# A second MLP's input projection by seven block products instead of eight, with its weights streamed from DRAM

## The chip, the cores and the metric

The kernel runs on one core of a Trainium2 chip. The metric is the device time of one execution in microseconds. Three runs of the kernel before took 1004.17, 1005.59 and 1006.8 us; the median is 1005.59.

## The reference

Three stages follow each other, all in float32. The third is the one that is rewritten.

```python
# attention: q, k, v (4, 8, 576, 64); a query sees its own and the 63 keys before it
x = attention(q, k, v)                       # then seen as (2304 tokens, 512)
# first MLP: 512 -> 1536 -> 512, gated
xn = x / sqrt(mean(x*x) + 1e-6) * rms_g
g = xn @ w_gate
x = (g * sigmoid(g) * (xn @ w_val)) @ w_out
# second MLP: 512 -> 2048 -> 512
h = x @ w_in
out = (h * sigmoid(1.702 * h)) @ w_out2
```

The weights arrive as 64-bit numbers and are turned into float32 on the chip.

## The kernel before, in words

**Precision.** Every large matmul is made of three: an operand is split into a high part (rounded to the matmul's float32r format) and a low part (the rest), and high x high, low x high and high x low are added up in PSUM. So a 128x128 weight tile is used in three matmuls per slice of tokens.

**Tiling.** 2304 tokens are 6 blocks of 384 (`TB`, `NB`). Activations are kept transposed: 512 features are 4 tiles of 128 partitions, tokens run along the free dimension. The first MLP goes over the 6 blocks twice (`ps_i`, each half with 6 of its 12 hidden tiles), since not all its weights fit beside each other; the second half adds to the result of the first (`part`) and evicts it (`x2s`) to DRAM (`x2d`).

**The second MLP, lines 685 to 738.** For each of the 6 blocks, for each of 16 hidden tiles of 128 features: `proj` (L428) does 12 matmuls of 384 columns into `psh` (4 feature tiles by 3 terms); the gate follows, sigmoid on ACT (L711), product on DVE (L712), high part on ACT (L715), low part on DVE (L716); `emit_P` then does 9 matmuls of 512 columns of the hidden tile before (3 slices of 128 tokens by 3 terms) into three accumulators. `psh` alternates between two PSUM banks. At a block's end the accumulators are copied to `ost` (two buffers) and stored.

**Weights.** `w_step` (L149) takes a pair of weight tiles from the queue `w_order`: a load into `st`, two operations on ACT, three on DVE (the conversion), and one step later `w_half` (L139) splits the pair into high and low parts in one of 16 buffers of 8 KB per partition (pool `wp`). The steps are spread by hand over the hidden tiles of the blocks (`extras`, L601). For the second MLP all 32 tiles (16 pairs) then stay in these 16 buffers until the end.

**What sets the order.** A scheduler places the instructions of each engine and assigns buffers; matmuls that go through `on_pe` while `pinned[0]` is set keep the order of the program. All large transfers go through one queue, SP's, in order. PSUM has 8 banks: 4 accumulators, 2 for projections (tags `g` and `v`), 2 for attention.

Of the kernel before, what the change touches and what calls it, by code (L numbers as in the profile page):

```python
# [22 lines left out]
def window_attention__gated_mlp__mlp_kernel(  # L23
# [86 lines left out]
    w_order += [(("h", 0), ("h", 1))]  # L110
    for f in range(2, NF2, 2):
        w_order += [(("h", f), ("h", f + 1)), (("p", f - 2), ("p", f - 1))]
    w_order += [(("p", NF2 - 2), ("p", NF2 - 1))]
# [24 lines left out]

    def w_half():  # L139
        if not half:  # L140
            return
        pair, w24 = half.pop()
        w = wp.tile([128, 2, 1024], F32R, tag="w", name="w")
        nc.scalar.copy(w[:, 0, :], w24.bitcast(F32))
        nc.vector.tensor_tensor(w[:, 1, :], w24.bitcast(F32), w[:, 0, :].bitcast(F32), ALU.subtract)
        for e, key in enumerate(pair):
            weights[key] = w[:, :, e * 512:(e + 1) * 512]
# [380 lines left out]
    if True:  # L528
# [52 lines left out]
        for ps_i in range(2):  # L581
            f_lo, f_hi = ps_i * FH, (ps_i + 1) * FH
            for j in range(NB):
# [17 lines left out]
                def extras(f, i):  # L601
                    s = 3 * (f - f_lo) + i
                    if ps_i == 0:
                        for fn in slots.pop(j * NS + s, ()):
                            fn()
                        if j == 0:
                            if s % 2 == 0:
                                w_step(n_wh)
                        elif s % 9 == 8:
                            w_step(n_w1)  # L610
                    elif not end:
                        if s % 9 == 2:
                            w_step(n_w)
                    else:
                        w_step(n_w)

                pend = None
                for f in range(f_lo, f_hi):
# [33 lines left out]
                    if f == f_lo:  # L652
                        if ps_i == 0 and end:
                            at_es.close()
                            x2p = ctx.enter_context(tc.tile_pool(name="x2p", bufs=1))
                            xr = raw_load(xd[0])
                        elif ps_i == 1:
                            xr = raw_load(x2d[0] if end else xd[j + 1])
# [3 lines left out]
                    if f == f_lo + 3 and (ps_i or end):  # L662
# [16 lines left out]
                if ps_i == 0 and 0 < j and not end:  # L679
# [5 lines left out]
        for i in range(NB):  # L685
            T = blocks2[i][1]
            NTC = T // 128
            acc = [acc_p.tile([128, 512], F32, tag=f"acc{c}", name=f"acc{c}") for c in range(NTC)]

            def emit_P(f, gh, gl):  # L690
                w = weights["p", f]
                terms = [(pi, c) for pi in range(3) for c in range(NTC)]
                if f == NF2 - 1:
                    terms = [(pi, c) for c in range(NTC) for pi in range(3)]
                for pi, c in terms:
                    nc.tensor.matmul(  # L696
                        acc[c],
                        (gh, gh, gl)[pi][:, c * 128:(c + 1) * 128],
                        w[:, (0, 1, 0)[pi], :],
                        start=(f == 0 and pi == 0),  # L700
                        stop=(f == NF2 - 1 and pi == 2),
                    )

            pend = None
            for f in range(NF2):
                while ("h", f) not in weights:
                    w_step(n_w)
                psh = mm_p.tile([128, 512], F32, tag="gv"[f % 2], name="psh")
                proj(psh, weights["h", f], xh, xl, T)
                a = ap_.tile([128, TB], F32, tag="a", name="a")  # L710
                nc.scalar.activation(a[:, :T], psh[:, :T], AF.Sigmoid, scale=1.702)  # L711
                nc.vector.tensor_tensor(a[:, :T], a[:, :T], psh[:, :T], ALU.mult)  # L712
                gh = ap_.tile([128, TB], F32R, tag="ah", name="gh")
                gl = ap_.tile([128, TB], F32R, tag="al", name="gl")
                nc.scalar.copy(gh[:, :T], a[:, :T])  # L715
                nc.vector.tensor_tensor(gl[:, :T], a[:, :T], gh[:, :T].bitcast(F32), ALU.subtract)  # L716
                if i == 0:
                    w_step(n_w)
                if pend is not None:
                    emit_P(*pend)  # L720
                pend = (f, gh, gl)
                if i == 0:
                    w_step(n_w)
                if i + 1 < NB:
                    if f == 2:
                        xr = raw_load(x2d[i + 1])
                    if f == 6:
                        nxh, nxl = raw_split(i + 1, xr)
            emit_P(*pend)
            xh, xl = nxh, nxl  # L730
            for c in range(NTC):
                st = stp.tile([128, 512], F32, tag="os", name="ost", bufs=2)
                if c % 2:
                    nc.vector.tensor_copy(st, acc[c])
                else:
                    nc.scalar.copy(st, acc[c])
                t0 = blocks2[i][0] + c * 128
                nc.sync.dma_start(out=out[t0:t0 + 128, :], in_=st)
# [30 lines left out]
```

## Time and profile before

| | |
|---|---|
| profiled execution, span | 1005.7 us |
| runs, median of 3 | 1005.59 us |
| PE busy | 978.5 us (97%) |
| DVE / ACT busy | 516.3 / 409.6 us |
| DMA | 88.44 MB, mean 88 GB/s |
| mean granted clock of PE | 0.986 |

The profile shows one execution; its span runs from the first to the last instruction, and it states no other time of its own. Three stretches can be told apart: attention with the first half of the first MLP to some 360 us, the second half of the first MLP to 591, and the second MLP to the end. Bytes moved by DMA fall to almost nothing in the last stretch, where all weights are on the chip.

### The profile page before, as it was taken

What the parts mean: (1) busy time and instruction counts of PE and PEld (TensorE: products, weight loads), DVE (VectorE), ACT (ScalarE), POOL (GpSimd) and SP (SyncE); (2) the same over time, 40 slices, a digit from 0 to 9 for tenths busy, and PEclk for the clock granted to TensorE, in tenths of its full rate; (3) what the DMA queues carried; (4) which work ended last, traced back from release to release, by engine and by line L of the source; (5) the groups of instructions that cost most, each with busy time, mean ns of one, the idle gap of its engine ahead of it and who ended that gap; (6) DMA issues with size and microseconds to landing.
All of it is one profiled execution on the core that took longest, in us unless ns stands there. A gap on an engine that the chain in (4) does not pass through costs nothing.

```text
span 1005.7 us, 15601 instructions
## 1 busy us (share of the span) xinstructions
PE 978.5 (97%) x6218; PEld 915.4 (91%) x6218; DVE 516.3 (51%) x1132; ACT 409.6 (41%) x884; POOL 12.2 (1%) x39
## 2 busy tenths in 40 slices
PE   8889999999998999999999999999999999999997
PEld 7888998889998999999999998998999989989996
DVE  5887667676766455665543787242322422322222
ACT  7786565656552333333322464232222322322222
POOL 2000000000000000000000000000000000000000
PEclk9899899999998999999999999999999999999999
DMA  9867445463525231341330541010010100000000
GB/s 223 244 182 207 116 112 155 103 163 101 146 85 168 74 106 45 134 148 73 136 128 9 171 147 50 1 63 1 8 56 1 53 11 1 32 1 1 32 1 32
DMA packets 113321, 88.44 MB, mean 88 GB/s; under 512 B 77664, under 2 KB 104288, under 8 KB 113248
## 3 DMA queue, kind: packets, MB, share of 16 engines
q1 hardware_dynamic: 112720, 87.44, 29.6%
q8 instruction: 49, 0.80, 0.3%
q14 instruction: 24, 0.20, 0.1%
q10 hardware_dynamic: 528, 0.00, 0.0%
HBM read 68.55 MB, written 18.87 MB: 87 GB/s over the span
## 4 chain that ended last, share of the span: by engine, by line
PE 87%; DVE 4%; DMA 3%; SPq 2%; ACT 2%; issue 1%; POOL 0%; DVEq 0%; ACTq 0%
PE acc L696 20%; PE psh L91 20%; PE psg L91 14%; PE psv L91 14%; PE acc L91 14%; SPq L225 2%; PE ps_s L91 1%; PE ps_v L91 1%; PE ps_t L91 1%; DMA qkv<-in_q_dram 1%; SPq L133 1%; DVE m L166 1%; PE ps_r L91 1%; DMA st<-in_moe_w_val_dram 1%; ACT p L321 1%
## 5 line engine op out<-in xcount | busy, mean ns | idle before, releaser
L712 DVE TENSOR_TENSOR a<-a,psh 128x384 f32<-128x384 f32 x96 | 53.1, 554 | 202.2 <-ACT a L711 202.2
L91 PE MATMUL psh<-x2h,w 128*128 128x384 f32 x768 | 153.2, 339 | 0.1
L696 PE MATMUL acc<-w,gh 128*128 128x512 f32 x576 | 152.9, 397 | 0.0
L91 PEld LDWEIGHTS psh<-x2h,w 128*128 128x128 f32 x768 | 137.2, 188 | 3.2 <-DVE a L712 0.4
L711 ACT ACTIVATE a<-psh 128x384 f32<-128x384 f32 x96 | 47.1, 492 | 220.4 <-PE psh L91 217.3
L696 PEld LDWEIGHTS acc<-w,gh 128*128 128x128 f32 x576 | 107.0, 188 | 18.5
L91 PE MATMUL acc<-ah,w 128*128 128x384 f32 x576 | 117.4, 342 | 1.0 <-DVE x2s L673 1.0
L91 PEld LDWEIGHTS acc<-ah,w 128*128 128x128 f32 x576 | 101.5, 188 | 2.7 <-DVE x2s L673 1.3
L627 DVE SCALAR_TENSOR_TENSOR a<-a,psg 128x384 f32<-128x384 f32 x72 | 39.8, 553 | 92.2 <-ACT a L624 92.1
L91 PE MATMUL psh<-x2l,w 128*128 128x384 f32 x384 | 86.2, 338 | 0.0
L696 PE MATMUL acc<-w,gl 128*128 128x512 f32 x288 | 85.1, 396 | 0.0
L716 DVE TENSOR_TENSOR gl<-a,gh 128x384 fp32r<-128x384 f32 x96 | 53.4, 557 | 50.5 <-ACT gh L715 42.7
L624 ACT ACTIVATE a<-psg 128x384 f32<-128x384 f32 x72 | 35.3, 490 | 102.5 <-PE psg L91 102.5
L91 PE MATMUL psg<-xh,w 128*128 128x384 f32 x288 | 70.2, 369 | 6.6 <-ACT xh L423 4.2
L91 PEld LDWEIGHTS psh<-x2l,w 128*128 128x128 f32 x384 | 69.9, 188 | 5.9
L715 ACT CAST gh<-a 128x384 fp32r<-128x384 f32 x96 | 49.3, 513 | 62.6 <-DVE a L712 49.8
L634 ACT CAST ah<-a 128x384 fp32r<-128x384 f32 x72 | 36.9, 513 | 81.9 <-DVE a L631 81.7
L696 PEld LDWEIGHTS acc<-w,gl 128*128 128x128 f32 x288 | 54.2, 189 | 12.5
L91 PE MATMUL acc<-al,w 128*128 128x384 f32 x288 | 63.9, 341 | 0.0
L91 PE MATMUL psv<-xh,w 128*128 128x384 f32 x288 | 62.0, 348 | 0.0
L91 PEld LDWEIGHTS psg<-xh,w 128*128 128x128 f32 x288 | 52.1, 199 | 10.8 <-ACT xh L423 5.0
L91 PE MATMUL psv<-x2h,w 128*128 128x384 f32 x288 | 58.9, 340 | 0.0
(106 smaller groups left out, 1413.4 us busy)
## 6 DMA issues: line engine op xcount, KB each, us to landing
st<-in_moe_w_out_dram SPq DMA_DIRECT2D x28, 512.0 KB, 4.4
o<-x2s SPq DMA_DIRECT2D x48, 192.0 KB, 2.0
st<-in_moe_w_in_dram SPq DMA_DIRECT2D x16, 512.0 KB, 4.6
st<-in_moe_w_gate_dram SPq DMA_DIRECT2D x12, 512.0 KB, 4.0
st<-in_moe_w_val_dram SPq DMA_DIRECT2D x12, 512.0 KB, 5.4
qkv<-in_v_dram SPq DMA_DIRECT2D x20, 256.0 KB, 3.9
x<-xraw SPq DMA_DIRECT2D x6, 768.0 KB, 3.5
xr<-x SPq DMA_DIRECT2D x6, 768.0 KB, 4.2
```

Source lines behind the costliest of these rows:

```text
L91: ins = op(*args, **kw)
L133: nc.sync.dma_start(out=dst, in_=w_src(kind, f))
L166: nc.vector.scalar_tensor_tensor(m.bitcast(U32), hi.bitcast(U32), 0x80000000, m.bitcast(U32), ALU.bitwise_and, ALU.bitwise_or)
L225: nc.sync.dma_start(out=t[off:off + n], in_=src[b, :, s:s + n, :].rearrange("h s d -> s h d"))
L624: tanh = nc.scalar.activation(a, psg[:, :T], AF.Tanh, scale=0.5).ins
L627: nc.vector.scalar_tensor_tensor(a, a, 1.0, psg[:, :T], ALU.add, ALU.mult)
L634: ah_ins = nc.scalar.copy(ah, a).ins
L696: nc.tensor.matmul(acc[c], (gh, gh, gl)[pi][:, c * 128:(c + 1) * 128], w[:, (0, 1, 0)[pi], :], start=(f == 0 and pi == 0), stop=(f == NF2 ...
L711: nc.scalar.activation(a[:, :T], psh[:, :T], AF.Sigmoid, scale=1.702)
L712: nc.vector.tensor_tensor(a[:, :T], a[:, :T], psh[:, :T], ALU.mult)
L715: nc.scalar.copy(gh[:, :T], a[:, :T])
L716: nc.vector.tensor_tensor(gl[:, :T], a[:, :T], gh[:, :T].bitcast(F32), ALU.subtract)
```

## The change

The input projection of the second MLP is rewritten as a product of 2x2 block matrices: two blocks of tokens (rows) by two halves of the 512 features, times two halves of the features by two hidden tiles (`f` and `f + 8`). Strassen's scheme (in Winograd's form) needs seven products of such blocks where the plain way has eight; each is 2 feature tiles by 3 terms, 6 matmuls of 384 columns. Sums and differences of the blocks are formed ahead of the split into high and low parts: of the weights in the first MLP (`w_products`, seven 256-column products per pair of hidden tiles, stored to DRAM as `wid`; the output weights are stored as `wod`), of the tokens once per pair of blocks (`x_operand`, seven operands in `wp` buffers).

The second MLP is now 3 pairs of blocks by 8 rounds. A round loads its weights from DRAM (`wi_load`, `wo_load`, one round ahead), accumulates products in two banks `a` and `b`, and takes copies of partial sums (`snapshot`) to form four gates. The output matmuls of the round before stand between the products, as four groups of nine (`groups`); the first round of a pair of blocks has two groups empty, or all but one in the very first, which gets the first MLP's last output matmuls (`late`). The accumulators are now six banks. PE's order is that of the program.

Shortened diff of the parts that matter:

```diff
-    w_order += [(("h", 0), ("h", 1))]
-    for f in range(2, NF2, 2):
-        w_order += [(("h", f), ("h", f + 1)), (("p", f - 2), ("p", f - 1))]
+    NP2 = NF2 // 2
+    for f in range(NP2):
+        w_order += [(("h", f), ("h", f + NP2)), (("p", f), ("p", f + NP2))]
...
+    def w_products(f, m):
+        b11, b21, b12, b22 = (m[:, i * 256:(i + 1) * 256] for i in range(4))
+        t = wp.tile([128, 4, 256], F32, tag="w", name="wt")
+        nc.vector.tensor_tensor(t[:, 0, :], b12, b11, ALU.subtract)
+        nc.vector.tensor_tensor(t[:, 1, :], b22, t[:, 0, :], ALU.subtract)
+        nc.vector.tensor_tensor(t[:, 2, :], b22, b12, ALU.subtract)
+        nc.vector.tensor_tensor(t[:, 3, :], b21, t[:, 1, :], ALU.subtract)
+        hi = wp.tile([128, 7, 256], F32R, tag="w", name="whi")
+        lo = wp.tile([128, 7, 256], F32R, tag="w", name="wlo")
+        for dst, src in ((slice(0, 2), m[:, 0:512]), (slice(2, 3), m[:, 768:1024]), (slice(3, 7), t)):
+            src = src if src is t else src.rearrange("p (b c) -> p b c", c=256)
+            nc.scalar.copy(hi[:, dst, :], src)
+            nc.vector.tensor_tensor(lo[:, dst, :], src, hi[:, dst, :].bitcast(F32), ALU.subtract)
+        d = dram.tile([128, 2, 7, 256], F32, name=f"wi_{f}", tag=f"wi_{f}")
+        nc.sync.dma_start(out=d[:, 0], in_=hi.bitcast(F32))
+        nc.sync.dma_start(out=d[:, 1], in_=lo.bitcast(F32))
+        wid[f] = d
...
-                    elif not end:
-                        if s % 9 == 2:
-                            w_step(n_w)
-                    else:
+                    elif s % 6 == 2:
                         w_step(n_w)
...
-                if ps_i == 0 and 0 < j and not end:
+                if (ps_i == 0 and 0 < j and not end) or (ps_i and end):
                     late.append(finish)
...
+        pinned[0] = True
...
+        def x_operand(raws, i):
...
+            t = wp.tile([128, 2, 2, TB], F32R, tag="w", name="xop")
+            nc.scalar.copy(t[:, 0], src)
+            nc.vector.tensor_tensor(t[:, 1], src, t[:, 0].bitcast(F32), ALU.subtract)
+            return t
...
+        def wi_load(f):
+            w = [wp.tile([128, 7, 256], F32R, tag="w", name="wi") for _ in range(2)]
+            for e in range(2):
+                nc.sync.dma_start(out=w[e].bitcast(F32), in_=wid[f][:, e])
+            return w
...
+        def product(ps, w, x, first):
+            i = 0
+            for wi, xx in ((0, 0), (1, 0), (0, 1)):
+                for c in range(2):
+                    on_pe(
+                        nc.tensor.matmul,
+                        ps[:, :TB],
+                        w[wi][:, c * 128:(c + 1) * 128],
+                        x[:, xx, c, :],
+                        start=(first and i == 0),
+                        stop=(i == 5),
...
+        def gate(c, g, i):
+            a = ap_.tile([128, TB], F32, tag="a", name="a")
+            nc.scalar.activation(a, c, AF.Sigmoid, scale=1.702)
+            nc.vector.tensor_tensor(a, a, c, ALU.mult)
+            nc.scalar.copy(g[0][:, i, :], a)
+            nc.vector.tensor_tensor(g[1][:, i, :], a, g[0][:, i, :].bitcast(F32), ALU.subtract)
...
+        def evict(sb, row):
+            if row % 3 == 0:
+                ost[0] = stp.tile([128, 3, 512], F32, tag="st", name="ost")
...
+            if f < NP2 - 1:
+                return [lambda q=q: terms([(q, c) for c in range(3)]) for q in (0, 3, 1, 2)]
+            return [lambda: None, lambda: rows(0), lambda: None, lambda: rows(1)]
...
+        groups = [late.pop()] + [lambda: None] * 3
+        for sb in range(NSB):
+            for f in range(NP2):
...
+                if not last:
+                    nwi, nwo = wi_load(f + 1), wo_load(f + 1)
+                elif sb + 1 < NSB:
+                    nwi, nwo = wi_load(0), wo_load(0)
+                if sb + 1 < NSB:
+                    if f == 2:
+                        raws = x_raws(sb + 1)
+                    if f in (4, 5, 6):
+                        i = MADE[f - 4]
+                        nxops[i] = x_operand(raws, i)
...
+                a = mm_p.tile([128, 512], F32, tag="g", name="psa")
+                prod(a, 0, True)
+                s1 = snapshot(a, "ah")
+                groups[0]()
...
+                prod(b, 1, True)
+                prod(a, 5, False)
+                nc.vector.tensor_tensor(s1, s1, b[:, :TB], ALU.add)
+                s2 = snapshot(a, "ah")
+                gate(s1, g, 0)
+                groups[1]()
...
+                prod(b, 6, True)
+                prod(a, 4, False)
+                s4 = snapshot(a, "al")
+                nc.vector.tensor_tensor(s4, s4, b[:, :TB], ALU.add)
+                gate(s4, g, 3)
+                groups[2]()
+                prod(a, 2, False)
+                prod(b, 3, False)
+                gate(a[:, :TB], g, 1)
+                nc.vector.tensor_tensor(s2, s2, b[:, :TB], ALU.add)
+                gate(s2, g, 2)
+                groups[3]()
+                groups = out_groups(sb, f, g, wo)
...
+            if sb + 1 < NSB:
+                for i in MADE[3:]:
+                    nxops[i] = x_operand(raws, i)
```

Where the instructions stand now, at three places. First PE, as the second MLP begins: before, two hidden tiles of block 0 and then the output matmuls of the first (psh is the projection, acc_6152 and acc_6153 two accumulators).

```order
L91 MATMUL psh<-x2h,w 128x384 x8
L91 MATMUL psh<-x2l,w 128x384 x4
L696 MATMUL acc_6152<-w,gh 128x512 x2
L696 MATMUL acc_6153<-w,gh 128x512 x2
L696 MATMUL acc_6152<-w,gl 128x512
L696 MATMUL acc_6153<-w,gl 128x512
```

The same place after the change, from the first MLP's last matmul on (psa and psb are the two banks of products, xop an operand of tokens, wi one of weights, wo the output weights).

```order
L91 MATMUL acc_5975<-al,w 128x384
L91 MATMUL psb<-xop,wi 128x384 x6
L91 MATMUL psa<-xop,wi 128x384 x6
L91 MATMUL psb<-xop,wi 128x384 x6
L91 MATMUL psa<-xop,wi 128x384 x12
L91 MATMUL psb<-xop,wi 128x384 x6
L91 MATMUL psa<-xop,wi 128x384 x6
L91 MATMUL acc<-wo,g 128x512 x9
```

In this first round no output matmuls stand between the products, and two products into bank a follow each other (x12); from the second round on there is a group of nine after the first, third, fifth and seventh product.

Second ACT, in the last block of the first MLP's second half. Before (psg is the gate's projection, ah the high part of the gated hidden tile, w the split of a weight pair, st its conversion):

```order
L624 ACTIVATE a<-psg 128x384
L144 CAST w<-m 128x1024
L634 CAST ah<-a 128x384
L163 ACTIVATE st<-st 128x1024
L164 ACTIVATE st<-st 128x1024
```

After, in the same block (L648 is the tanh, L658 the cast ah, L744 the high parts of the first pair's operands):

```order
L166 CAST w<-m 128x1024
L744 CAST xop<-xr 128x768 x2
L744 CAST xop<-xs 128x768 x2
L648 ACTIVATE a<-psg 128x384
L658 CAST ah<-a 128x384
L744 CAST xop<-xs 128x768 x2
L648 ACTIVATE a<-psg 128x384
L744 CAST xop<-xr 128x768
L658 CAST ah<-a 128x384 x2
```

Four operand casts and the tanh of the next hidden tile now stand between a weight cast and the cast ah.

Third the queue of SP, around the last stores of the first MLP (o_5 is the last block's result). Before:

```order
L450 DMA xr<-o_2_5101 128x1536
L133 DMA st<-in_moe_w_out_dram 128x1024 x2
L676 DMA o_5_6139<-x2s 128x384 x4
L450 DMA xr<-o_3_5432 128x1536
```

After (wi and wo are the streamed weights of a round):

```order
L753 DMA wi<-wi_4280 128x1792 x2
L758 DMA wo<-wo_4397 128x2048
L719 DMA xr<-o_3_5568 128x1536
L753 DMA wi<-wi_4530 128x1792 x2
L758 DMA wo<-wo_4641 128x2048
L753 DMA wi<-wi_4767 128x1792 x2
L758 DMA wo<-wo_4891 128x2048
L700 DMA o_5_6300<-x2s 128x384 x4
```

The loads of the first three rounds stand ahead of the four stores.

## Rows read from the trace of the kernel before

**Rows 1.** The page's first part: busy us, share of the span, instructions, by engine.

```profile
PE 978.5 (97%) x6218; PEld 915.4 (91%) x6218; DVE 516.3 (51%) x1132; ACT 409.6 (41%) x884; POOL 12.2 (1%) x39
```

**Rows 2.** Busy us of each engine (instructions) by stretch, PE clock, DMA share, GB/s.

```profile
362.00:591.40 229.40, 229.40 (x1299) 228.96 (x1298) 130.76 (x213) 81.85 (x125) 0.00 (x0) 1.00 0.33 112
562.00:574.00 12.00, 12.00 (x70) 12.00 (x69) 10.83 (x16) 3.70 (x6) 0.00 (x0) 1.00 0.56 186
591.40:1000.00 408.60, 408.30 (x2030) 367.84 (x2028) 139.86 (x247) 115.77 (x222) 0.00 (x0) 1.00 0.07 24
```

**Rows 3.** The page's groups: line, engine, operation, tiles, count, busy us, mean ns, idle.

```profile
L91 PE MATMUL psh<-x2h,w 128*128 128x384 f32 x768 | 153.2, 339 | 0.1
L696 PE MATMUL acc<-w,gh 128*128 128x512 f32 x576 | 152.9, 397 | 0.0
...
L91 PE MATMUL psh<-x2l,w 128*128 128x384 f32 x384 | 86.2, 338 | 0.0
L696 PE MATMUL acc<-w,gl 128*128 128x512 f32 x288 | 85.1, 396 | 0.0
...
L715 ACT CAST gh<-a 128x384 fp32r<-128x384 f32 x96 | 49.3, 513 | 62.6 <-DVE a L712 49.8
```

**Rows 4.** Timeline, second MLP: start us, us, engine, line, operation, count, idle before.

```profile
703.15 0.87 PE L91 MATMUL psh<-x2l,w 128*128 128x384 f32 x4
...
703.86 1.57 PE L91 MATMUL psh<-x2h,w 128*128 128x384 f32 x8
704.12 0.49 ACT L711 ACTIVATE a<-psh 128x384 f32<-128x384 f32 x1 [2.60 <-PE psh L91]
...
705.27 1.57 PE L696 MATMUL acc<-w,gh 128*128 128x512 f32 x6
...
706.68 0.86 PE L696 MATMUL acc<-w,gl 128*128 128x512 f32 x3
...
707.38 0.87 PE L91 MATMUL psh<-x2l,w 128*128 128x384 f32 x4
```

**Rows 5.** Groups by shape, 362 to 591.4 us, DVE and ACT.

```profile
L166 DVE SCALAR_TENSOR_TENSOR m<-st,m 128x1024 uint32<-128x1024 uint32 x12 | 14.7, 1222 | 0.2
L169 DVE CUSTOM_DVE_ANT_0 m<-st,m 128x2048 uint16<-128x2048 uint16 x12 | 14.6, 1218 | 0.1
...
L144 ACT CAST w<-m 128x1024 fp32r<-128x1024 f32 x12 | 12.6, 1050 | 19.8 <-DVE m L169 18.1 <-PE psv L91 1.6
...
L671 DVE SCALAR_TENSOR_TENSOR x2s<-acc,part 128x384 f32<-128x384 f32 x20 | 10.5, 553 | 4.0 <-PE acc L91 3.0 <-DMA o<-x2s 0.8
L165 DVE TENSOR_SCALAR m<-st 128x1024 uint32<-128x1024 uint32 x12 | 8.3, 692 | 3.8 <-ACT st L163 3.8
```

**Rows 6.** DMA issues: queue, count, KB each, us from issue to landing.

```profile
xr<-o SPq DMA_DIRECT2D x6, 768.0 KB, 4.1
```

**Rows 7.** Timeline of the end.

```profile
998.93 0.86 PE L696 MATMUL acc<-w,gl 128*128 128x512 f32 x3
...
1002.10 0.59 ACT L736 COPY ost<-acc 128x512 f32<-128x512 f32 x1 [2.15 <-DMA out_dram<-ost]
1002.71 0.33 SPq L738 DMA_DIRECT2D out_dram<-ost  x1
```

**Rows 8.** Busy us by stretch, where PE's clock fell and where not.

```profile
320.00:322.00 2.00, 2.00 (x7) 2.00 (x8) 2.00 (x4) 0.00 (x0) 0.00 (x0) 0.50 0.98 280
333.50:336.00 2.50, 1.50 (x7) 0.99 (x6) 1.48 (x3) 0.95 (x3) 0.00 (x0) 1.00 0.23 81
```

**Rows 9.** Timeline of PE around these two places.

```profile
318.03 0.44 PE L91 MATMUL psg<-xh,w 128*128 128x384 f32 x1 [1.30 <-ACT xh L423]
319.89 2.61 PE L91 MATMUL psg<-xh,w 128*128 128x384 f32 x7 [1.42 <-DVE xh L421]
...
335.20 1.15 PE L91 MATMUL acc<-ah,w 128*128 128x384 f32 x5 [0.99 <-DVE x2s L673]
```

More of the change, by code (lines that the diff above doesn't have):

```diff
@@ L145, in w_half @@
         nc.vector.tensor_tensor(w[:, 1, :], w24.bitcast(F32), w[:, 0, :].bitcast(F32), ALU.subtract)
+        if pair[0][0] == "p":
+            d = dram.tile([128, 2, 1024], F32, name=f"wo_{pair[0][1]}", tag=f"wo_{pair[0][1]}")
+            nc.sync.dma_start(out=d, in_=w.bitcast(F32))
+            wod[pair[0][1]] = d
+            return
         for e, key in enumerate(pair):
@@ L656, in window_attention__gated_mlp__mlp_kernel @@
                             xr = raw_load(xd[0])
-                        elif ps_i == 1:
-                            xr = raw_load(x2d[0] if end else xd[j + 1])
+                        elif ps_i == 1 and not end:
+                            xr = raw_load(xd[j + 1])
                     if f == f_lo + 1 and ps_i == 1:
@@ new lines, in window_attention__gated_mlp__mlp_kernel, with x_raws @@
+        while w_next[1] < n_w or half:
+            w_step(n_w)
+        pinned[0] = True
+        W_OF = (0, 1, 2, 6, 3, 4, 5)
+        NSB = NB // 2
+        def x_raws(sb):
+            r = [x2p.tile([128, KC, TB], F32, tag=t, name="xr") for t in ("xr", "xh")]
+            for e in range(2):
+                nc.sync.dma_start(out=r[e], in_=x2d[2 * sb + e])
+            sums = x2p.tile([128, 2, 2, TB], F32, tag="xl", name="xs")
+            return [r[0][:, 0:2, :], r[0][:, 2:4, :], r[1][:, 0:2, :], r[1][:, 2:4, :], sums[:, 0], sums[:, 1]]
@@ new lines, in window_attention__gated_mlp__mlp_kernel, with out_term @@
+        accs = {}
+        def out_term(sb, f, g, wo, q, c, pi):
+            e, t = q % 2, q // 2
+            row = 3 * t + c
+            on_pe(
+                nc.tensor.matmul,
+                accs[sb][row],
+                g[(0, 0, 1)[pi]][:, q, c * 128:(c + 1) * 128],
+                wo[:, (0, 1, 0)[pi], e * 512:(e + 1) * 512],
+                start=(f == 0 and q == 3 * t and pi == 0),
+                stop=(f == NP2 - 1 and q == 1 + t and pi == 2),
+            )
+        def evict(sb, row):
+            if row % 3 == 0:
+                ost[0] = stp.tile([128, 3, 512], F32, tag="st", name="ost")
+            st = ost[0][:, row % 3, :]
+            if row % 2:
+                nc.vector.tensor_copy(st, accs[sb][row])
+            else:
+                nc.scalar.copy(st, accs[sb][row])
+            t0 = sb * 2 * TB + row * 128
+            nc.sync.dma_start(out=out[t0:t0 + 128, :], in_=st)
@@ new lines, in window_attention__gated_mlp__mlp_kernel, with out_groups, terms, rows @@
+        ost = [None]
+        def out_groups(sb, f, g, wo):
+            def terms(todo):
+                for q, c in todo:
+                    for pi in range(3):
+                        out_term(sb, f, g, wo, q, c, pi)
+            def rows(t):
+                for c in range(3):
+                    terms([(3 * t, c), (1 + t, c)])
+                    evict(sb, 3 * t + c)
+            if f == 0:
+                banks = [(acc_p, f"acc{c}") for c in range(4)] + [(atp, "att")] * 2
+                accs[sb] = [pool.tile([128, 512], F32, tag=tag, name="acc") for pool, tag in banks]
+            if f < NP2 - 1:
+                return [lambda q=q: terms([(q, c) for c in range(3)]) for q in (0, 3, 1, 2)]
+            return [lambda: None, lambda: rows(0), lambda: None, lambda: rows(1)]
@@ L742 @@
+        for fn in groups:
+            fn()
 _INS = ["q", "k", "v", "moe_w_gate", "moe_w_val", "moe_w_out", "moe_rms_g", "moe2_w_in", "moe2_w_out"]
```

103 lines of the change are left out of this document (52 added, 51 removed).

## The prediction

> **What bounds the kernel now.** I read the page's first part, then the busy time by stretch, then the costliest groups, then the timeline of a few microseconds in the stretch that the change rewrites. The first part shows PE busy for 978.5 of 1005.7 us [rows 1]; the next busiest engine has half of that. A busy PE may still be waiting inside its pipeline, so the share alone says little. The stretch of the second MLP, 591.4 to 1000, says more: PE 408.3 of 408.6 us at clock 1.00, DVE 140, ACT 116, DMA 24 GB/s [rows 2]. The groups give the count of its matmuls: 768 + 384 into psh with 384 columns, 576 + 288 into acc with 512 [rows 3]. The duration of one (339 or 397 ns) is a latency and overlaps its neighbours; the price is the distance between starts. In the timeline [rows 4] 12 matmuls of 384 go from 703.15 to 705.27, 0.1767 us each, and 9 of 512 from 705.27 to 707.38, 0.2344 each: one hidden tile of one block takes 4.23. 96 of these are 406.1; the 12 matmuls of 384 columns that the first MLP leaves to this stretch are 2.1; together 408.2 of 408.6. So there is nothing in it but the matmul stream, and a matmul less is its whole distance less, as long as nothing else comes late.
>
> **The change, part by part.** *Products.* A round (two blocks, two hidden tiles) had 48 input matmuls and has seven products of six: 42. There are 24 rounds, so 144 fewer: 144 x 0.1767 = -25.4 us. The output matmuls stay at 864. A new round lasts 42 x 0.1767 + 36 x 0.2344 = 15.86 us. Six-matmul runs cost nothing extra by the same rows: the change from 384 to 512 columns and back is already inside the 4.23.
>
> *Element work in the round.* Three copies on ACT and three additions on DVE come to four gates. No row shows a copy out of a product's bank; the nearest are the gate's cast on ACT, 0.51 [rows 3], and an eviction of 384 columns on DVE, 0.55 [rows 5]. With these DVE has 11 x 0.55 = 6.1 and ACT 11 x 0.5 = 5.5 of 15.86 us, so neither is a bound. What counts is the chain on one bank: PE's last matmul, copy, next product into the same bank. The sigmoid starts 0.26 after PE's next matmul (703.86 to 704.12) [rows 4]; with 0.49 for the copy and an estimated 0.1 until PE goes on it is 0.85. Between a copy and the next product into that bank stand nine output matmuls (2.11) or another product (1.06), so it is hidden, at 0. That cover is missing in the first round of each of the three block pairs, where the group before the third product into bank a is empty, as the order on PE shows (psa x12): 3 x 0.85 = +2.55. In the very first round the second round's first product also waits for the gate that reads bank a, 0.26 + 0.49 + 0.55 + 0.1 = 1.4 behind six matmuls of 1.06, with evictions of the first MLP ahead of it on DVE: +1.0, between 0 and 5 (below, the queue).
>
> *Streamed weights.* A round loads 2 x 0.917 + 1.049 = 2.88 MB, 182 GB/s for 15.86 us. Nothing of before streams so long, but from 562 to 574 the DMA moved 186 GB/s at a share of 0.56, so about 330 at full share, while PE was busy for all 12 us at clock 1.00 and DVE for 10.8 [rows 2]. A load of 768 KB lands 4.1 us after its issue [rows 6]. The 16 weight buffers hold seven operands, the round's three tiles, the output tile of the round before and the next three: 14, so the loads run a round ahead. I put it at 0, between 0 and +10 at the changes of block pair, where the next pair's operands take the spare buffers.
>
> *Preparation in the first MLP.* Each of eight pairs of hidden tiles gets four 256-column subtractions and 768 more columns of low parts on DVE. With 0.55 at 384 columns and 1.22 at 1024 [rows 5] that is 4 x 0.42 + 1.11 = 2.8, 22 in all; of DVE's 140 us in the second MLP 107 are gates (192 x 0.555), and of the other 33 I count half as weight work that moves here; eleven 768-column operations (0.95 each by the same two rows) make the first operands. DVE goes from 131 [rows 2] to about 180 of 229 us. Its 90% beside a PE without a gap from 562 to 574 [rows 2] lets me put this at 0, with one exception, which the order on ACT shows: in the last block a weight cast, four operand casts and the next tanh stand ahead of the cast ah. After the tanh DVE must do 0.55 + 0.69 + 1.22 + 2 x 0.55 + 1.22 = 4.8 before the weight cast can start; then ACT has 1.05 + 4 x 0.83 (estimated between 0.51 and 1.05) + 0.49 + 0.51 = 5.4 [rows 3, 5]. With 0.75 until the tanh is done and 0.1 to PE this is 11.0; PE has 48 matmuls, 8.5 us, before it needs ah. A wait of 2.5, and 0.5 for the gate that comes late behind it: +3.0, between 0 and 8.
>
> *The end.* Before, the three last accumulators are complete within one group, the third copy waits 2.15 for a transfer to free one of two buffers, and the span ends 6.07 after the last matmul (998.93 + 3 x 0.2344 = 999.63). From the last transfer's issue it is 2.99 [rows 7]. After, rows complete six matmuls apart into tiles of three rows in three buffers: 0.26 + 0.6 for the copy + 2.99 = 3.85. -2.2.
>
> *Sum.* -25.4 + 2.55 + 1.0 + 3.0 - 2.2 = -21.0 on the span of 1005.7: 984.7. The median of the runs, 1005.59, is 0.1 under that span, so I make no other allowance.
>
> **The rivals.** *The clock falls.* After two waits of 1.3 and 1.4 us in the 3 us before 320 [rows 9], PE ran at 0.50 [rows 8], the lower of its two levels (1.2 instead of 2.4 GHz), and seven matmuls from 319.89 on took 2.61 us where six distances of 0.1767 and one latency of 0.34 would be 1.4. I put such an event at some 3 us. A single wait of 1.0 before 335.20 left the clock at 1.00 [rows 8, 9]. The Trainium skill says the same ("TensorE: Matmul & The Clock Gate", Part 1): the array's clock is halved unless it has been busy, and idle stretches bring the half rate back; the trace agrees, 0.50 after the two waits. The new waits of 0.85 stand alone; those of the last block (2.5, then 0.5) and of the first round (0.85, then 1.0) are pairs. For it: these two; against it: the wait at 335. Price 3 us an event, one to four events: 988 to 997. Chance 0.10.
>
> *The queue of loads.* On SP the loads of rounds 1 and 2 stand ahead of the first MLP's last four stores, as the order shows, and those stores free the two buffers in which DVE evicts. 5.8 MB at 330 GB/s are 17 us. If they are all issued just before the stores, DVE stands behind them, and so does the gate that frees bank a: about +10, or the same in pieces at the two changes of block pair: 990 to 997. For it: one queue in order. Against it: buffers come free one by one through the last block, so most of these loads are issued earlier. Chance 0.09.
>
> *The stream is too slow (slower than before).* If loads came at less than 2.88 MB in 15.86 + 21.0/24 = 16.7 us, 172 GB/s, the gain would be gone; at 160 GB/s a round is 18.0 us and the time 984.7 + 24 x 2.15 = 1036. For it: before never streams like this; from 362 to 591 the mean was 112 GB/s [rows 2]. Against it: that took a share of 0.33, again some 340 at full share, and the stream has nothing else on its queue. Chance 0.04.
>
> *No new wait shows.* Then only products and end count: 1005.7 - 25.4 - 2.2 = 978. The overlap of neighbouring DVE instructions speaks for it in the last block; the missing cover in the first rounds against it. Chance 0.10.
>
> *The page's pace.* The Trainium skill ("TensorE: Matmul & The Clock Gate", Back-to-back issue gap) gives 81 ns for 128 and 131 ns for 512 columns in a stream with weight loads, so an estimate of 114 for 384; by it the products would save 16.4 us and the sum be 993.7. Rows 4 have 176.7 and 234.4 in this very stretch, and I go by them.
>
> **How the numbers follow.** The forecast, 981 to 989, has 0.67; the clock 0.10, the queue 0.09, no wait 0.10, the slow stream 0.04. The likeliest gives 984.7. The range reaches from "no wait" to the upper ends of the first two rivals, 978 to 996, and leaves out the slow stream and a little of the rest. About 0.3% (3 us) is what a measurement of this kernel can tell from no change. Faster by more holds in all cases but the slow stream, 0.95 with a little taken off; no change needs that stream near its threshold, 0.01; slower 0.04.
>
> **What would show it.** Right: from the first product to the last matmul about 385 us instead of 408 at clock 1.00, 1008 matmuls of 384 columns at 0.177 apart, PE's idle time in three waits just under 1 us for the copy after the third pair of products and one of 2 to 3 us for ah in the first MLP's last block, and under 4 us from last matmul to end. DMA at about 180 GB/s through the second MLP, share a little above one half. Wrong: products waiting for wi or wo, a granted clock of 0.5 anywhere after 580, gaps in PE between 362 and 580, or matmuls further apart beside the stream.

## The result and the profile after

The changed kernel takes 982.62 us (median of four runs, 981.10 to 984.83), against 1006.19 for the kernel before in the same set of runs: a ratio of 0.977 (95% interval 0.976 to 0.979). The forecast was 984.7, in a range of 978 to 996. The profiled execution has a span of 982.8 us, 22.9 less than that of before. The page's first part [rows 1] now reads:

```profile
PE 952.2 (97%) x6074; PEld 888.6 (90%) x6074; DVE 585.3 (60%) x1252; ACT 459.9 (47%) x978; POOL 12.2 (1%) x39
```

144 matmuls are gone, DVE has 69 us and ACT 50 us more work, and PE is still the engine that is busy all the time. Two stretches, busy us of each engine with instructions, then PE clock, DMA share and GB/s [rows 2]: the first is the part of the first MLP in which the second's weights are prepared, the second lies within the second MLP.

```profile
362.00:580.00 218.00, 214.99 (x1214) 214.02 (x1213) 166.00 (x272) 98.83 (x148) 0.00 (x0) 1.00 0.68 244
640.00:978.00 338.00, 336.86 (x1663) 300.72 (x1663) 147.41 (x259) 129.01 (x254) 0.00 (x0) 1.00 0.48 179
```

The second row has what was foretold for the round: clock 1.00, DMA at 179 GB/s (share 0.48, where a little above one half was foretold), and PE busy for all but 1.1 of 338 us. The first row is no longer full: 3 us of PE are missing there. The waits of PE from 540 us on (what waited, for whom, us in total, times, longest) say where everything that is lost lies:

```profile
PE acc L91 <- ACT ah L658: 2.0, 1, 2.0
PE psa L91 <- ACT snap L785: 1.7, 3, 0.6
PE psa L91 <- DVE a L779: 1.2, 1, 1.2
PE psv L91 <- DVE a L655: 1.0, 1, 1.0
```

In this order: the high part ah of a gate in the first MLP's last block; the copy out of bank a, once in the first round of each pair of blocks; the gate's multiplication that reads bank a, ahead of the second round's first product; and a multiplication in the first MLP's last block that has to free a bank. No product and no output matmul ever waits for wi or wo. The view counts a wait from the modelled end of the matmul before; measured as distance between starts beyond the usual distance, the same waits are 2.12, 3 x 0.73 (0.84 with the slower matmul behind each), 1.32 and 1.16 us.

The page's groups for the three products-and-output lines [rows 3], and the timeline of PE over a third of a round [rows 4]:

```profile
L91 PE MATMUL acc<-wo,g 128*128 128x512 f32 x864 | 215.9, 395 | 0.0
...
L91 PE MATMUL psa<-xop,wi 128*128 128x384 f32 x576 | 116.5, 336 | 2.9 <-ACT snap L785 1.7
...
L91 PE MATMUL psb<-xop,wi 128*128 128x384 f32 x432 | 87.1, 336 | 0.0
```

```profile
704.39 1.21 PE L91 MATMUL psb<-xop,wi 128*128 128x384 f32 x6
705.45 1.21 PE L91 MATMUL psa<-xop,wi 128*128 128x384 f32 x6
706.49 2.26 PE L91 MATMUL acc<-wo,g 128*128 128x512 f32 x9
708.59 1.21 PE L91 MATMUL psb<-xop,wi 128*128 128x384 f32 x6
```

Twelve matmuls of 384 columns take 2.10 us from 704.39 to 706.49, 0.175 each where [rows 4] had 0.1767; nine of 512 take 2.10, 0.233 instead of 0.2344. Over the whole second MLP the means from one start to the next, waits left out, are 0.1747 after a matmul of 384 columns and 0.2334 after one of 512, where the kernel before has 0.1764 and 0.2342. That was not in the forecast.

At the end the last copy no longer waits for a transfer (last matmul's group, the last two copies) [rows 7]:

```profile
976.83 2.27 PE L91 MATMUL acc<-wo,g 128*128 128x512 f32 x9
...
977.73 0.59 ACT L809 COPY ost<-acc 128x512 f32<-128x512 f32 x1 [2.23 <-PE acc L91]
979.13 0.69 DVE L807 COPY ost<-acc 128x512 f32<-128x512 f32 x1 [2.12 <-PE acc L91]
```

The span ends 3.9 us after the last matmul (978.93), where it was 6.07.

### The profile page after: what moved, and what is told of

The parts are those of the page before. It is cut to its first block, busy times and chain, and to the rows that moved or that the text cites. A ratio compares the mean times of both kernels' runs of the same rounds, so it can differ in the third digit from the quotient of the medians.

```text
span 982.8 us, 15649 instructions
## 1 busy us (share of the span) xinstructions
PE 952.2 (97%) x6074; PEld 888.6 (90%) x6074; DVE 585.3 (60%) x1252; ACT 459.9 (47%) x978; POOL 12.2 (1%) x39
## 4 chain that ended last, share of the span: by engine, by line
PE 85%; DVE 6%; DMA 3%; ACT 3%; SPq 2%; issue 1%; POOL 0%; DVEq 0%; ACTq 0%
PE acc L91 34%; PE psg L91 14%; PE psv L91 13%; PE psa L91 10%; PE psb L91 7%; PE ps_v L91 2%; PE ps_s L91 1%; SPq L252 1%; PE ps_t L91 1%; PE ps_r L91 1%; DMA o<-x2s 1%; ACT st L190 1%; DMA st<-in_moe_w_out_dram 1%; DMA wi<-wlo 1%; DVE m L193 1%
## 5 line engine op out<-in xcount | busy, mean ns | idle before, releaser
L91 PE MATMUL acc<-wo,g 128*128 128x512 f32 x864 | 215.9, 395 | 0.0
L91 PEld LDWEIGHTS acc<-wo,g 128*128 128x128 f32 x864 | 161.7, 188 | 31.7
L91 PE MATMUL psa<-xop,wi 128*128 128x384 f32 x576 | 116.5, 336 | 2.9 <-ACT snap L785 1.7
L91 PEld LDWEIGHTS psa<-xop,wi 128*128 128x128 f32 x576 | 102.1, 188 | 7.7 <-ACT snap L785 2.7
L91 PE MATMUL psb<-xop,wi 128*128 128x384 f32 x432 | 87.1, 336 | 0.0
L91 PEld LDWEIGHTS psb<-xop,wi 128*128 128x128 f32 x432 | 77.1, 188 | 3.7
L781 DVE TENSOR_TENSOR g<-a,g 128x384 fp32r<-128x384 f32 x96 | 53.2, 557 | 40.8 <-ACT g L780 38.9
L651 DVE SCALAR_TENSOR_TENSOR a<-a,psg 128x384 f32<-128x384 f32 x72 | 39.7, 551 | 63.2 <-ACT a L648 62.9
L648 ACT ACTIVATE a<-psg 128x384 f32<-128x384 f32 x72 | 35.2, 489 | 88.4 <-PE psg L91 88.4
L658 ACT CAST ah<-a 128x384 fp32r<-128x384 f32 x72 | 37.0, 513 | 74.2 <-DVE a L655 74.1
L780 ACT CAST g<-a 128x384 fp32r<-128x384 f32 x96 | 49.3, 514 | 45.9 <-DVE a L779 45.9
L348 ACT ACTIVATE p<-p,sm 128x128 f32<-128x128 f32 x128 | 49.6, 391 | 20.5 <-DVE sm L336 20.5
L91 PE MATMUL psg<-x2h,w 128*128 128x384 f32 x288 | 56.8, 339 | 0.1
```

The costliest lines, as they stand in the source:

```text
L91: ins = op(*args, **kw)
L348: last_exp[0] = nc.scalar.activation(p[e][:, hp, :], p[e][:, hp, :], AF.Exp, bias=sm[:, 0, i:i + 1], scale=-1.0, accum_out=sm[:, 1, i:i + ...
L648: tanh = nc.scalar.activation(a, psg[:, :T], AF.Tanh, scale=0.5).ins
L651: nc.vector.scalar_tensor_tensor(a, a, 1.0, psg[:, :T], ALU.add, ALU.mult)
L658: ah_ins = nc.scalar.copy(ah, a).ins
L780: nc.scalar.copy(g[0][:, i, :], a)
```

## The experiments

Times of different sets of runs are compared through the kernel before, which ran in each; its median moved between 1005.2 and 1007.2. A run's part before 340 us, which the change does not touch, takes up to 3 us more or less from one execution to the next, so single profiles are compared by stretches, each from start to start: from the first product (before: the first psh) to the last matmul, "the second MLP", 383.6 us in the changed kernel and 407.8 before; and from the first matmul of the first MLP's second half to there, 232.8 and 229.2.

**One product twice.** `prod(b, 1, True)` is issued two times in a row.

```
                 prod(b, 1, True)
+                prod(b, 1, True)
                 prod(a, 5, False)
```

> Theory (the second MLP holds nothing but the matmul stream, so products are what the change gains): one product of each round computed twice, 144 matmuls of 384 columns more, no other work: 144 x 0.175 = +25.2 us over the changed kernel, 1007.8. Rival A (the gain came from something else, PE has slack in a round that other engines or the loads fill): 983 to 990. Rival B (a matmul more in a round costs what it did in before, 0.1766, the shorter distance of 0.1746 being due to the order of the new round): 144 x 0.1766 = 25.4 and the distance of the others back at 0.1766, 1010.

1007.78 us, a ratio of 1.0027 (1.0016 to 1.0038) to before, so 25.5 over the changed kernel by way of the ratios. In the trace the second MLP takes 408.0 us, 24.4 more, while its waits sum to 0.6 us less (the one for DVE a is 0.9 shorter, and 0.3 is lost ahead of it); 25.0 / 144 is 0.173 for each matmul added. The theory holds: a matmul put in costs its whole distance. The mean distance stays at 0.1745, so rival B is out too.

**More loads.** One or three further loads of 1.05 MB a round go into buffers that nobody reads.

```
             nc.sync.dma_start(out=w.bitcast(F32), in_=wod[f])
+            for _ in range(1):      # 3 in the second kernel
+                xt = stp.tile([128, 2, 1024], F32, tag='st', name='xt')
+                nc.sync.dma_start(out=xt, in_=wod[f])
```

> Each round loads another 1.05 MB into a buffer that nobody reads: 3.93 MB in 15.8 us, 249 GB/s instead of 182. Theory (the streamed weights cost nothing and have room left): 982 to 984, no PE wait for wi or wo, matmuls no further apart. Rival (the stream is near its limit, or its traffic spaces the matmuls): waits for wi or wo in most rounds, or distances up by 1% and more; at a limit of 200 GB/s a round of 19.7 us and 1076.

> Each round loads another 3.15 MB into buffers that nobody reads: 6.03 MB a round, which would need 382 GB/s at 15.8 us. Theory (the load stream has a ceiling of 330 to 373 GB/s at full share, and the changed kernel is at half of it): a round of 16.2 to 18.3 us, so +10 to +60: 993 to 1043, with PE waiting for wi or wo. Rival (no ceiling in reach, the loads hide even so): 983 to 985.

987.23 (0.9825, 0.9811 to 0.9838) and 993.59 (0.9883, 0.9869 to 0.9896): 5 and 11 us over the changed kernel, above what the theory gave for the first and at the lower edge for the second. But it is not the rate. Stretches with three more loads, at the start of the second MLP and later:

```profile
600.00:612.00 12.00, 3.15 (x15) 2.21 (x13) 4.38 (x8) 2.33 (x5) 0.00 (x0) 0.78 1.01 418
640.00:970.00 330.00, 327.81 (x1622) 293.04 (x1621) 145.22 (x256) 127.05 (x250) 0.00 (x0) 1.00 0.89 352
```

From 640 on PE is busy for 1.1 us less than without them, at 352 GB/s; at full share the DMA moves 418 GB/s here, not the 330 estimated in the forecast. What is lost is lost at one place. With three more loads, PE's longest wait and the line of DVE behind it in the timeline:

```profile
PE acc L91 <- DVE x2s L695: 10.9, 1, 10.9
```

```profile
614.12 1.02 DVE L695 SCALAR_TENSOR_TENSOR x2s<-acc,part 128x384 f32<-128x384 f32 x2 [9.17 <-DMA o<-x2s]
```

and with one:

```profile
PE acc L91 <- DVE x2s L695: 6.4, 1, 6.4
```

```profile
608.42 1.03 DVE L695 SCALAR_TENSOR_TENSOR x2s<-acc,part 128x384 f32<-128x384 f32 x2 [4.53 <-DMA o<-x2s]
```

These are the evictions of the first MLP's last results, which wait until the stores of the first two have left their buffers; those stores share the DMA with the loads, and land up to 15.4 us after their issue with one load more and 17.0 with three, 5.8 in the changed kernel. This is the forecast's rival "the queue of loads", and near its +10. Only its last step is another: PE does not wait for the gate that frees bank a (that wait is 0.2 and 0.7 us here, 1.2 in the changed kernel), but for the evictions themselves, whose accumulator banks the output matmuls need. And behind the wait the clock falls, here with one load more (the stretches ahead of it and behind it, then PE's timeline there):

```profile
600.00:602.50 2.50, 2.50 (x12) 1.97 (x12) 2.50 (x6) 1.29 (x3) 0.00 (x0) 1.00 1.01 419
608.80:611.80 3.00, 2.76 (x8) 2.47 (x9) 0.66 (x2) 0.00 (x0) 0.00 (x0) 0.50 1.01 416
```

```profile
609.04 1.65 PE L91 MATMUL acc<-wo,g 128*128 128x512 f32 x3 [6.45 <-DVE x2s L695]
610.48 2.12 PE L91 MATMUL psb<-xop,wi 128*128 128x384 f32 x6
```

Six products take 2.12 us where they took 1.21 in the round shown above; the clock is 0.68 from 611.8 to 613 and 1.00 from there to 616. The matmuls at the lower clock cost 1.7 us (2.7 with three more loads); with 6.6 for the wait, and the wait for DVE a 1.0 shorter, that is the 7.4 us by which the second MLP is longer here (391.0).

The runs show less than that for one load more, 5 us, because something was won ahead of the second MLP: the stretch before it takes 229.5 us, and 229.2 with three more loads, instead of 232.8. The two waits in the first MLP's last block are all but gone. In these two kernels the instructions of that block stand in another order too, so the loads are not all that changed. On ACT, with one load more, the cast ah comes first:

```profile
559.55 0.51 ACT L658 CAST ah<-a 128x384 fp32r<-128x384 f32 x1
560.45 1.05 ACT L166 CAST w<-m 128x1024 fp32r<-128x1024 f32 x1 [0.39 <-DVE m L196]
```

With three more loads the second MLP is 14.6 longer (398.2) and the stretch ahead of it 3.6 shorter: the 11 us of the runs.

**The end alone, in the kernel before.**

```
-                st = stp.tile([128, 512], F32, tag="os", name="ost", bufs=2)
+                if c == 0:
+                    ost = stp.tile([128, 3, 512], F32, tag="st", name="ost")
+                st = ost[:, c, :]
```

> The kernel before, with its output evictions put into one buffer of three rows as in the changed kernel, nothing else. Theory (the third copy waited 2.15 us for a transfer to free one of two buffers): the end comes 2.15 us earlier, 1003.4 against 1005.6, and 3.9 us after the last matmul. Rival (the last transfers are the end, whenever the third copy starts): no change, 1005.6.

1004.82 against 1005.22, a ratio of 0.9996 (0.9987 to 1.0005): by the runs no difference that can be told, at most 1.3 us. The trace shows why it is not 2.15. The third copy starts at once:

```profile
999.50 1.07 ACT L738 COPY ost<-acc 128x512 f32<-128x512 f32 x2 [2.07 <-PE acc L696]
999.74 0.69 DVE L736 COPY ost<-acc 128x512 f32<-128x512 f32 x1 [1.71 <-PE acc L696]
1000.11 1.31 SPq L740 DMA_DIRECT2D out_dram<-ost  x3
```

but the three transfers are now issued within 1.3 us, and the last lands 2.5 us after its issue instead of 2.0. The end comes 4.7 us after the last matmul, not 3.9. So in this trace 1.4 of the 2.2 us are the buffers, a little more than the runs allow. The other 0.8 are put down to the rows that complete six matmuls apart, which only the new order of the output has; no run tried that by itself.

**The groups of the pairs' last rounds spread over the next round.**

```
+            if sb + 1 < NSB:
+                return [lambda: terms([(0, c) for c in range(3)]), lambda: rest(0),
+                        lambda: terms([(3, c) for c in range(3)]), lambda: rest(1)]
             return [lambda: None, lambda: rows(0), lambda: None, lambda: rows(1)]
```

(`rest(t)` gives the second term of each row of block t and evicts it.)

> The changed kernel, with the output groups of the last round of the first two block pairs put into all four places of the next round (three rows after its second product pair, three at its end) instead of two of them; work and counts the same. Theory (PE waits 0.84 us for the copy of bank a wherever the group ahead of the third product into it is empty): the waits at 726 and 853 us are gone, that at 602 stays: -1.7 us, 981. Rival (the wait comes from the evictions or the operand work at the change of pair, not from the missing cover): the same two waits at another place, no change in time, 982.6.

980.65 (ratio 0.9744, 0.9728 to 0.9761). The second MLP takes 381.9, 1.7 less as expected, and PE waits for the copy once instead of three times:

```profile
PE psa L91 <- ACT snap L785: 0.6, 1, 0.6
```

The wait hangs on the nine output matmuls that were missing in front of it.

**The first operands behind the first gate of the last block.**

```
-            xops[i] = x_operand(raws, i)
+            with after(ah_0), after(al_0):      # ah, al of the last block's first hidden tile
+                xops[i] = x_operand(raws, i)
```

> The changed kernel, with the first block pair's operands (casts on ACT, sums and low parts on DVE) issued behind the first ah and al of the first MLP's last block. Theory (in that block the operand work stands ahead of the gate on ACT and DVE): the waits at 561.5 (1.2 us, for DVE) and 564.9 (2.1, for ACT) go, the first product comes 3 us earlier, 979.5. Rival A (the weight steps on DVE are enough to make the gate late): the wait for DVE stays and that for ACT falls, -2.1. Rival B (the operands then come late for the first product, or make the next gates late instead): 0 to -1, 982.

980.54 (0.9735, 0.9714 to 0.9757), 3.8 us less than the changed kernel by way of the ratios. Both waits before the first product are gone, and a new one has come (all waits of PE from 540 on):

```profile
PE psa L91 <- ACT snap L787: 1.7, 3, 0.6
PE acc L91 <- DVE x2s L697: 1.0, 1, 1.0
PE psa L91 <- DVE a L781: 0.2, 1, 0.2
```

The wait of 1.3 behind DVE a in the first round became one of 1.1 behind the same two evictions at another place. So the piling up in the last block was the cause, on ACT and DVE; the stretch up to the first product takes 229.1 us instead of 232.8, as long as before the change.

**The last results in place.** The first MLP's last four results go into the tile of partial sums, so that no store frees a buffer.

```
-   st = stp.tile([128, TB], F32, tag="os", name="x2s", bufs=2)
+   st = ... if not (ps_i and end) else part[:, c, :]
```

> The changed kernel, with the first MLP's last four results written over the partial sums that they are added to, so that no eviction waits for a store to free a buffer. Theory (the wait of 1.3 us before the second round's first product comes from two evictions on DVE that stand behind stores landing 4 to 5 us after their issue, beside the loads): DVE evicts at once, the wait at 605.3 falls to about 0.4, -1 us, 981.6. Rival (it is the gate's own chain of sigmoid, multiplication and bank, which six matmuls don't cover): the wait stays at 1.3, 982.6.

984.74 (0.9783, 0.9764 to 0.9802): no gain. The wait for DVE a falls from 1.3 to 0.35 as the theory said, and the one before the fourth product into bank a grows from 0.73 to 1.84. On ACT the changed kernel, then this one:

```profile
596.40 0.48 ACT L785 COPY snap<-psa 128x384 f32<-128x384 f32 x1 [2.13 <-PE psa L91]
596.90 1.28 ACT L778 ACT_TABLE_LOAD   x1
600.19 0.53 ACT L778 ACTIVATE a<-snap 128x384 f32<-128x384 f32 x1 [2.00 <-DVE snap L868]
```

```profile
598.25 0.48 ACT L785 COPY snap<-psa 128x384 f32<-128x384 f32 x1 [3.69 <-PE psa L91]
598.75 1.28 ACT L778 ACT_TABLE_LOAD   x1
600.04 0.52 ACT L778 ACTIVATE a<-snap 128x384 f32<-128x384 f32 x1
```

The load of the sigmoid's table, 1.28 us, lay in ACT's idle time; with the new order of the program it stands behind the second copy, in the chain that frees bank a. Neither theory nor rival had this.

**The three together, and two repairs.** First the three edits as they are:

> The three edits together (output groups spread over the round, first operands behind the first gate of the last block, last results written in place). Theory (the waits are independent): -1.7 - 3 - 1 = -5.7, 977, which is the 978 of the rival without new waits less the shorter distance of the matmuls and plus the one wait left. Rival (removing one makes another longer, since the same DVE and ACT work lies there): -2 to -3, 980.

978.40 (0.9723, 0.9707 to 0.9739): the waits in the second MLP sum to 2.2 us, not the 1.1 of the theory, with the table load and DVE's sums for the next pair's operands in the way. So a kernel with a sigmoid that nobody reads right behind the first copy, and the next pair's operands held back, with the changed kernel beside it:

```
                 s1 = snapshot(a, "ah")
+                if sb == 0 and f == 0:
+                    early = ap_.tile([128, TB], F32, tag="a", name="early")
+                    nc.scalar.activation(early, s1, AF.Sigmoid, scale=1.702)
...
-                        nxops[i] = x_operand(raws, i)
+                        with after(hi_f), after(lo_f):   # last gate of the round before
+                            nxops[i] = x_operand(raws, i)
```

> The changed kernel once more, beside the next two: 982.6, so that their differences can be read within one set of runs. Both theories: the same waits in the second MLP as in its first profile, and only the part before 340 us moving by 1 to 3 us from one execution to the next.

> The three edits of the run before them (groups spread, first operands behind the first gate, last results in place), and two more: one sigmoid without a reader right behind the first copy out of bank a, and the operands of the next block pair held behind the gate of the round before. Theory (with the last results in place the wait before the third product into bank a grew from 0.73 to 1.84 because the table load of 1.28 us for the sigmoid moved from idle time into the chain of the first gate, and in the run of all three the sums of the second pair's operands, 2 x 0.95 on DVE, stood ahead of the first addition): of the waits 0.89, 0.97 and 0.34 after the first product 0.73 and about 0.35 are left, the stretch from first product to last matmul falls from 382.1 to 381.0 and the time is 977.3. Rival (the wait comes from the four evictions of 1.95 us on DVE ahead of the first addition, not from the table): one wait of 1.5 to 2 stays, 978.4.

983.40 for the changed kernel (0.9775, 0.9758 to 0.9791; the same waits in its second MLP, 383.5 us) and 976.70 for this one (0.9702, 0.9688 to 0.9716): 6.7 us faster than the changed kernel, 30 than before. Its second MLP takes 380.9, and these are all its waits from 540 on:

```profile
PE psa L91 <- ACT snap L788: 0.6, 1, 0.6
PE psa L91 <- DVE a L781: 0.2, 1, 0.2
```

The four evictions of the rival still take 1.95 us on DVE in this kernel, ahead of the first addition, and the wait for the copy is 0.73 all the same; so they were not its cause. The two repairs were run only together: what each is worth by itself is not shown.

**The order of the matmuls, in the kernel before.**

```
-        for wi, xx in ((0, xh), (1, xh), (0, xl)):
-            for c in range(KC):
+        for wi, xx, c in [(wi, xx, c) for h in (0, 2)
+                for wi, xx in ((0, xh), (1, xh), (0, xl)) for c in (h, h + 1)]:
```

> The kernel before, with the twelve matmuls of every input projection in the order that a pair of products has: high by high, low by high and high by low of the first two 128-row chunks, then of the other two, instead of four chunks at a time. Theory (the shorter distance of the products, 0.1746 instead of 0.1766, comes from the order of the matmuls): 0.1746 here too, 2304 x 0.002 = -4.6 us, 1001. Rival (it comes from where the weights lie or how they got there, or from the new round's element work): 0.1766 as before, 1005.6.

The distance does not change. Twelve matmuls of 384 columns, from the first row to the last:

```profile
710.03 0.52 PE L91 MATMUL psh<-x2h,w 128*128 128x384 f32 x2
...
712.15 0.64 PE L696 MATMUL acc<-w,gh 128*128 128x512 f32 x2
```

2.12 / 12 = 0.1767, as in [rows 4]; the mean over the second MLP is 0.1764, as before. So the order is not the cause of the shorter distance. The time is 1016.03 (1.0094, 1.0077 to 1.0111), 9 us longer. In the profile it is 6.9, of which 6.8 lie before the second MLP, which starts at 598.4 instead of 591.6: the same function serves the first MLP, where attention is interleaved. Why that part grew was not followed up.

## Why the prediction was right

The sum of the forecast was -21.0 on the span; -22.9 was measured. By its terms:

| term | forecast | measured | from |
|---|---|---|---|
| 144 matmuls fewer | -25.4 | -25.4 | 144 x 0.1764, the mean before; e1: 144 more cost 25.0 at the shorter distance |
| first round of each pair | +2.55 | +2.5 | 3 x 0.84 |
| second round's first product | +1.0 | +1.4 | 1.32, and 0.1 behind it |
| last block of the first MLP | +3.0 | +3.5 | the stretch up to the second MLP, 232.8 and 229.2 before; two waits are 3.3 of it |
| end | -2.2 | -2.2 | 3.9 after the last matmul, 6.07 before |
| streamed weights | 0 | 0 | no wait for wi or wo |
| shorter distances | - | -2.4 | 1008 x 0.00174 + 864 x 0.00074 |
| a wait that the kernel before had | - | -0.4 | for DVE a (L712), before the matmul at 598.2 |

Before rounding the terms sum to -22.8, so nothing is left over.

*Products.* The second MLP was a full stream, so what is taken out is gained whole; putting the same number of matmuls back brings the time to 1007.8.

*First rounds.* Each of the three waits is 0.84 where 0.85 was worked out from a sigmoid's start behind its last matmul, and spreading the output groups takes away exactly the two that it can. (Bank a takes four products in a round, 0, 5, 4 and 2; it is the fourth that waits, where the forecast says the third.)

*Last block.* The mechanism was as described, with two errors in the sum that cancel in part. The rows of ACT show the gate's ah behind a weight cast, four operand casts and a tanh, 4.8 us where 5.4 was worked out:

```profile
562.29 1.05 ACT L166 CAST w<-m 128x1024 fp32r<-128x1024 f32 x1 [4.21 <-DVE m L196]
563.25 1.56 ACT L744 CAST xop<-xr 128x768 fp32r<-128x768 f32 x2
564.72 1.56 ACT L744 CAST xop<-xs 128x768 fp32r<-128x768 f32 x2
566.18 0.48 ACT L648 ACTIVATE a<-psg 128x384 f32<-128x384 f32 x1
566.57 0.50 ACT L658 CAST ah<-a 128x384 fp32r<-128x384 f32 x1
```

On DVE two sums for the operands, 0.96 each, stand ahead of the gate's first multiplication (L651), the first of them held up by a load; the forecast's chain of 4.8 did not have them:

```profile
555.91 0.96 DVE L731 TENSOR_TENSOR xs<-xr 128x768 f32<-128x768 f32 x1 [2.46 <-DMA xr<-o]
556.90 0.96 DVE L734 TENSOR_TENSOR xs<-xs,xr 128x768 f32<-128x768 f32 x1
557.78 0.55 DVE L651 SCALAR_TENSOR_TENSOR a<-a,psg 128x384 f32<-128x384 f32 x1
```

From the end of the tanh (556.00) to the weight cast (562.29) it is 6.3 us, 1.5 more than worked out. So ah is 0.9 later than forecast, and PE waits for 3.3 instead of 2.5: 1.16 for DVE's multiplication (L655), which was not foreseen as a wait, and then 2.12 for ACT. Of the 0.5 for the next gate 0.2 came. That the term fits to 0.5 us is in part luck. The forecast also named gaps in PE between 362 and 580 as a sign of being wrong, though its own wait for ah falls there; that sign was ill chosen.

*Second round.* 1.4 instead of 1.0, and for the reason that was given to the rival: two evictions waited 0.95 us for a store to land, and the gate that frees bank a stood behind them.

```profile
604.64 0.49 ACT L778 ACTIVATE a<-psa 128x384 f32<-128x384 f32 x1 [0.32 <-PE psa L91]
604.71 1.05 DVE L695 SCALAR_TENSOR_TENSOR x2s<-acc,part 128x384 f32<-128x384 f32 x2 [0.95 <-DMA o<-x2s]
...
605.67 0.55 DVE L779 TENSOR_TENSOR a<-a,snap 128x384 f32<-128x384 f32 x1
606.14 0.55 DVE L779 TENSOR_TENSOR a<-a,psa 128x384 f32<-128x384 f32 x1
...
606.74 0.97 PE L91 MATMUL psa<-xop,wi 128*128 128x384 f32 x4 [1.16 <-DVE a L779]
```

*Streaming.* Right at 0, and with more room than was worked out: 418 GB/s at full share, and at 352 the rounds still keep their pace. The threshold of 172 GB/s in the rival of the slow stream was never near.

*The end.* Right in size, with a reason that holds only in part: the wait for a buffer is 1.4 of it in the trace, and the rest is put down to the spacing of the last rows.

*The rivals.* No event of the clock came: behind the waits of 1.0 and 2.0 us at 562.8 and 567.1, and the one of 1.2 at 606.7, it stayed at 1.00. The queue of loads was there in small, and took 6.4 and 10.9 us when the loads were made larger. "No new wait shows" was wrong, but its 978 is about where the kernel gets almost without them, 976.7: 2.4 less for the shorter distances, and 1.3 more for the two waits that are left.

*What failed* is the price of the matmuls that stay. The forecast took 0.1767 and 0.2344 from before for the new stream; they are 0.1747 and 0.2334, where the means before are 0.1764 and 0.2342: -2.4 us. That is more than the whole difference of 1.9 between forecast and result; the waits that were a little longer, +0.9, stand against it. So the forecast is as near as it is because errors on both sides cancel in part.

## What to carry to other kernels

Where one stretch is a full stream of matmuls, price a matmul less by the distance between starts and then look only for the places where the new program has less cover than the old: the first round after a change of stage, and the last block before it, where work of the next stage is pulled forward. A load stream that is hidden everywhere can still hold up a few small stores that share its DMA, when these free the buffers that an engine needs. And removing one wait can move a table load or a sum into the chain behind it, so look at each engine's order again after every repair.

## What was not expected of the hardware

- Matmuls of 384 columns start 0.1747 us apart in the new stream and 0.1764 in the old (means, waits left out), to 0.0002 in every profile of both. The extra product shows that it is not the number of matmuls in a row, the reordered kernel that it is not the order of high and low parts. In the kernel before the distance goes by the place among the twelve, from 0.1735 to 0.180 (means from 640 to 960 us), and the reordered kernel has the same at each place to 0.0002, with other operands there. The cause stays open; where the weights lie and how they came there were not tried.
- Behind one wait of 6.45 us the clock stood at 0.50, the lower of the two levels: the matmuls until it came back cost 1.7 us more, and 2.7 behind the wait of 10.9, where the forecast had some 3 for such an event. Behind waits of 1.0 and 2.0 us within 5 us of one another it stayed at 1.00.
- A transfer of 256 KB that shares the DMA with two others landed 2.5 us after its issue, and 2.0 alone; stores of 192 KB among the loads took up to 17.0.
